# Attention feeding a gated feed-forward block: the order of the early loads, two sets of casts, and the first weights in two pieces

## The chip, the core and the metric

The kernel runs on one core of a Trainium2 chip. The metric is the device time of one execution in microseconds (us), as the median of several runs; lower is better. The engines named below are TensorE (PE, and PEld for its weight loads), VectorE (DVE), ScalarE (ACT), GpSimd (POOL) and SyncE (SP), which here does nothing but issue transfers. GpSimd issues transfers too, on a DMA queue of its own.

## What is computed

Causal attention with a forgetting bias, over 8 batches of 8 heads, 576 positions and head size 64, and a gated feed-forward block on its output:

```
scores = (q @ k^T) / 8
cum    = cumsum(max(s, 0))
scores = where(causal, scores + min(-(cum_i - cum_j), 0), -1e9)
attn   = softmax(scores);  o = attn @ v
x      = o, heads side by side                   # 4608 tokens x 512
g      = x @ w_gate                              # 512 x 1536
out    = (g * sigmoid(g) * (x @ w_val)) @ w_out  # 1536 x 512
```

Inputs and output are float32; the matmuls run in bfloat16.

## The kernel before

**Tiles.** The 64 heads are numbered 0 to 63 (`bh` or `kk`), eight to a batch, four to a head block (`hb` or `h`, 0 to 15). One load brings k or q of a head block into a float32 buffer (`rawk`, `rawq`, 576 KB each, three buffers in turn). One load of V is a batch (`rawv`, five chunks of up to 128 positions, one buffer only). `cast_one` makes bfloat16 copies `ck` and `cq` of a head block (L249); `cast_v` makes those of V into `vt` (L176). k and q must lie transposed in `kq`, of which there are two sets, taken in turn by head blocks. For head blocks 0 to 4 TensorE transposes (L291) and ScalarE (k, L318) and VectorE (q, L320) copy the result into `kq`; `prep_one(hb, i)` does one of the four pieces of that. From block 5 on the casts are written to memory and come back through transposing transfers.

Four more rows of `kq` come from the cumulative sums, by small transfers (`aug`, L190), so that the score matmul adds the bias by itself.

**A head.** `score_piece` does the score matmuls in four pieces (L367), the exponential on ScalarE (L380) and the causal masks on GpSimd (L383 on the 512 columns of the diagonal, L388 on the last 64). `av_piece` multiplies by V, with a column of ones for the softmax sum (L405); `av_out` divides (L421, L422). The result goes transposed into `XT`: for the first two batches by TensorE (L455), later through memory.

**The feed-forward block** takes 512 tokens at a time (`ffn_items`, nine such tiles, 36 items each): twelve times a gate group of four matmuls (L571), tanh on ScalarE (L576), a value group (L586) and two VectorE operations, then four output groups of twelve matmuls (L599). The weights lie in `wg`, `wv` (two halves of 768 columns each) and `wo` (two halves), loaded by GpSimd with a cast on the way (L336).

**What sets the order.** [...] the order is written out by hand. `first_batch` does batch 0 alone (heads 0 to 7), with the first loads placed after chosen heads. Then the main loop goes through the items of the feed-forward tiles and between them calls `pump`, which advances the generator `attn_items` (heads 8 and on) to a set position. While the first feed-forward tile runs, the position goes from 8 to 17.65, linearly from item 6 to item 36. `hook` places single actions after numbered items of the first tile.

Within `attn_items`, `PREP_AT[h]` says after which (head of the block, score piece) a piece of the next head block's preparation comes. `side(h, step)`, called after the second score piece of a head, places later loads and casts: the casts of V 1 at head 11, those of head block 5 at heads 13 and 14, loads of V 2 at heads 10 and 11, of head block 6 at head 12. `AV_AT` puts the output matmuls of heads 8 and 9 after the scores of head 12, those of 10 and 11 after 13, those of 12 and 13 after 14. Since there is one `rawv` buffer, the load of V 2 can't begin before all casts of V 1 are done.

On SyncE's queue the program's order before is: V 0; k, q 2; rows of block 2; k, q 3; rows of block 3; V 1; k, q 4; V 2; k, q 6; k, q 5.

Of the kernel before, what the change touches and what calls it, by code (L numbers as in the profile page):

```python
# [19 lines left out]
def kernel(  # L20
# [11 lines left out]
    nc = tc.nc  # L32
# [48 lines left out]
    NPE = 5  # L81
# [24 lines left out]
    with tc.manual_schedule():  # L106
# [41 lines left out]
        def load_one(hb, name, rs=(0, NR)):  # L148
            b, g = divmod(hb, 2)
            if rs[0] == 0:  # L150
                loaded[name, hb] = raw.tile([128, NR, J, D], FP32, tag="raw" + name, name="raw" + name)
            nc.sync.dma_start(  # L152
                loaded[name, hb][:, rs[0] : rs[1], :, :].rearrange("x r j d -> x r (j d)"),
                SRC[name][0][b, g * HB + 2 * rs[0] : g * HB + 2 * rs[1], :, :].rearrange(
                    "(r e) (p j) d -> (e p) r (j d)", e=2, j=J
                ),
            )

        def load_qk(hb):
            load_one(hb, "k")  # L160
            load_one(hb, "q")

        def load_v(b, cs):
            if 0 in cs:
                loaded["v", b] = raw.tile([128, NCH, H, D], FP32, tag="rawv", bufs=1, name="rawv")
            t = loaded["v", b]
            for c in cs:
                n = 128 if c < 4 else TAIL
                nc.sync.dma_start(  # L169
                    t[0:n, c, :, :],  # L170
                    v[b, :, c * 128 : c * 128 + n, :].rearrange("h p d -> p h d"),
                )
# [12 lines left out]
        def aug(hb, engs):  # L185
            for hh in range(HB):
                r, e = divmod(hh, 2)
                r0 = 64 * (1 - r)
                bh = hb * HB + hh
                engs[hh].dma_start(  # L190
                    KQ[hb % 2][r][r0 : r0 + 4, :, e * S : (e + 1) * S],
                    HL[bh : bh + 1, :, :, :],
                )
# [48 lines left out]
        def cast_one(hb, name, eng):  # L242
            cts[name, hb] = cp.tile([128, J, NR, D], BF16, tag="c" + name, bufs=2, name="c" + name)
            dst = cts[name, hb].rearrange("x j r d -> x r j d")
            src_t = loaded[name, hb]
            if eng is nc.scalar:
                nc.scalar.copy(dst, src_t)
            else:
                eng.tensor_copy(dst, src_t)  # L249
# [75 lines left out]
        def w_load(kind, j, h=None):  # L325
            dst = {"g": WG, "v": WV, "o": WO}[kind][j]
            if kind == "o":
                src_ap = moe_w_out[j * WKO * 128 : (j + 1) * WKO * 128, :].rearrange(
                    "(c p) n -> p c n", p=128
                )  # L330
            else:
                w = moe_w_gate if kind == "g" else moe_w_val
                lo, hi = (0, WCH) if h is None else (h * WCH // 2, (h + 1) * WCH // 2)
                src_ap = w[:, j * WCH + lo : j * WCH + hi].rearrange("(c p) n -> p c n", p=128)
                dst = dst[:, :, lo:hi]
            nc.gpsimd.dma_start(dst, src_ap)  # L336
# [101 lines left out]
        def x_out(pr):  # L438
            nc.gpsimd.dma_start(  # L439
                XS[pr].rearrange("(c p) d -> p c d", p=128), ots.pop(pr)  # L440
            )
# [6 lines left out]
        def x_pe(pr, eng=None):  # L448
            b, r = divmod(pr, H // 2)
            ot = ots.pop(pr)  # L450
            bs = take()
            ps = view16(bs, S)
            for c in range(NCH):
                n = 128 if c < 4 else TAIL
                nc.tensor.transpose(  # L455
                    ps[:, c * 128 : c * 128 + n], ot[0:n, c, :], ident[0:n, 0:n]
                )
            for lo, hi, at in x_parts(b):
                if eng is nc.scalar:
                    nc.scalar.copy(XT[:, r, at : at + hi - lo], ps[:, lo:hi])  # L460
                else:
                    nc.vector.tensor_copy(XT[:, r, at : at + hi - lo], ps[:, lo:hi])
            give(bs)
# [40 lines left out]
        def prep_one(hb, i):  # L504
            g, nm = divmod(i, 2)
            nm = ("k", "q")[nm]
            pe_transpose(hb, nm, g)
            for r in range(2):
                pe_out(hb, nm, g, r, nc.scalar if nm == "k" else nc.vector)

        PREP_AT = {
            2: {(1, 3): 0, (2, 1): 1, (2, 3): 2, (3, 1): 3},
            3: {(0, 3): 0, (1, 3): 1, (2, 1): 2, (2, 3): 3},
        }

        AV_AT = {
# [5 lines left out]
        def attn_items():  # L522
            for kk in range(H, BH + 2):
                h, step = divmod(kk, HB)
                if kk < BH:
                    if step == 3 and h + 2 < NPE:
                        cast_one(h + 2, "k", nc.gpsimd)
                        cast_one(h + 2, "q", nc.gpsimd)
                    if step == 0 and 3 < h + 1 < NPE:
                        aug(h + 1, GP4)  # L530
                    for ci in range(4):
                        score_piece(kk, ci)
                        if ci == 1:
                            side(h, step)
                        yield kk + 0.1 + ci / 8
                        if (step, ci) in PREP_AT.get(h, ()):
                            prep_one(h + 1, PREP_AT[h][step, ci])
                            yield kk + 0.1 + ci / 8
                for x in X_AT.get(kk, (kk - 2,)):
                    if x % 2 == 1 and H <= x < BH:  # L540
                        if x < XB * H:
                            x_pe(x // 2)
                            yield kk + 0.5
                        else:
                            x_in(x // 2)
                for p in AV_AT.get(kk, (kk - 1,)):
                    if H <= p < BH:
                        av_piece(p, (0, 1, 2))
                        yield kk + 0.6
                        av_piece(p, (3,))  # L550
                        yield kk + 0.7
                        av_piece(p, (4,))
                        av_out(p)
                        if p >= XB * H and p % 2 == 1:
                            x_out(p // 2)
                        yield kk + 0.8
# [101 lines left out]
            give(bs)  # L658

        def first_batch():  # L660
            wq = {1: (("g", 0), ("v", 0)), 4: (("g", 1),), 5: (("v", 1),)}
            tail = {
                6: ("a0", "a1"),
                7: ("a2", "a3", "a4", "x0", "a5", "x1", "a6", "a7", "x2", "w6", "x3", "w8"),
            }
            for h in range(H):
                for ci in range(4):
                    score_piece(h, ci)
                for w in wq.get(h, ()):
                    w_load(*w)  # L670
                if h == 1:
                    order = [(nm, g) for g in range(2) for nm in ("k", "q")]
                    for nm, g in order:
                        pe_transpose(1, nm, g)
                    for r in range(2):
                        for nm, g in order:
                            pe_out(1, nm, g, r, nc.vector)
                    for c in range(3, 5):
                        cast_v(0, c, nc.vector)
                if h == 2:  # L680
                    for c in range(3):
                        cast_v(0, c, nc.gpsimd)
                if h == 3:
                    aug(2, SP4)
                    load_qk(3)
                if h == 7:
                    aug(3, SP4)
                    load_v(1, range(5))
                    load_qk(4)
                    cast_one(2, "k", nc.gpsimd)  # L690
                    cast_one(2, "q", nc.gpsimd)
                    w_load("o", 0)
                    w_load("o", 1)
                for what in tail.get(h, ()):
                    i = int(what[1:])
                    if what[0] == "a":
                        av_piece(i, range(NCH))
                        av_out(i)
                    elif what[0] == "x":
                        x_pe(i, nc.scalar)  # L700
                    else:
                        keep_warm(i)
# [6 lines left out]
        def pump(upto):  # L709
# [9 lines left out]
            2: [lambda: prep_one(2, 1)],  # L719
            3: [lambda: prep_one(2, 2)],  # L720
            4: [lambda: prep_one(2, 3)],
            9: [lambda: cast_one(3, "k", nc.gpsimd), lambda: cast_one(3, "q", nc.gpsimd)],
            21: [lambda: load_qk(5)],
        }
        for tt in range(NTT):
            lo = H * (tt + 1) + LAGS[tt]
# [40 lines left out]
```

The softmax here doesn't subtract the row's maximum and nothing guards it: scores larger than these inputs give would overflow.

## Time and profile before

The time is 401.94 us, the median of three runs (400.12 to 403.02). The profiled execution has a span of 401.8 us at a mean granted TensorE clock of 0.987.

| engine | busy us | share of the span |
|---|---|---|
| PE | 373.3 | 93% |
| PEld | 207.3 | 52% |
| DVE | 241.5 | 60% |
| ACT | 214.3 | 53% |
| POOL | 192.4 | 48% |

Some single operations that the text below uses:

| operation | line | engine | mean ns |
|---|---|---|---|
| feed-forward matmul, 512 columns | L571, L586, L599 | PE | 381 to 383 |
| exponential of 128x512 | L380 | ACT | 504 |
| mask on 512 columns | L383 | POOL | 644 |
| cast of k of a head block | L249 | POOL | 1148 |
| issue of one weight load | L336 | POOL | 757 to 840 |

The page has a row per engine with its busy share in 40 equal slices of the span, one with the clock that TensorE was granted and one with the share of the 16 DMA engines. Beside it, the list of waits says for an engine how long it waited, in how many times, and for what; the timeline gives instructions in order of time, with the idle time ahead of each and what ended it in brackets; and the busy time can be had for any stretch. Times of matmuls overlap, since they are pipelined, and the record leaves out a few of them.

### The profile page before, as it was taken

The numbers are of one execution on the slowest core, as the hardware profiler recorded it, in microseconds if no ns is written. First come the engines' busy times: TensorE is split into PE (matmuls) and PEld (weight loads), VectorE is DVE, ScalarE is ACT, GpSimd is POOL, SyncE is SP. The second block draws the span as 40 slices with busy tenths as digits, with TensorE's granted clock in tenths as the row PEclk, the third lists the DMA queues.
The fourth block names the chain that finished last, engine by engine and source line by source line (L and its number), as shares of the span: only waits on it lengthen the run. The fifth ranks groups of instructions, "written<-read, shape, count | busy, mean of one in ns | idle before, by whom it ended". The sixth has DMA issues, their size and how long they took to land.

```text
span 401.8 us, 7873 instructions
## 1 busy us (share of the span) xinstructions
PE 373.3 (93%) x2943; PEld 207.3 (52%) x2994; DVE 241.5 (60%) x431; ACT 214.3 (53%) x411; POOL 192.4 (48%) x329
## 2 busy tenths in 40 slices
PE   4789979399999999999999999999999999999996
PEld 3575535255555555555555555555555554444442
DVE  7766756315885578627962795479627743842850
ACT  8576954245765665556555655565556522323321
POOL 7581436176578675667565756575542211001001
PEclk9999989979999999999999999999999999999999
DMA  7999975689685998899389939793531114002002
GB/s 248 223 268 207 197 185 125 234 213 244 153 185 148 278 288 176 204 286 232 106 197 277 232 112 190 217 208 104 97 127 27 23 25 135 2 22 82 2 0 105
DMA packets 100534, 64.18 MB, mean 160 GB/s; under 512 B 81888, under 2 KB 85824, under 8 KB 100496
## 3 DMA queue, kind: packets, MB, share of 16 engines
q1 hardware_dynamic: 90672, 45.23, 47.2%
q0 software_dynamic: 9680, 18.32, 17.1%
q8 instruction: 23, 0.38, 0.4%
q14 instruction: 15, 0.12, 0.1%
q10 hardware_dynamic: 144, 0.13, 0.1%
HBM read 37.90 MB, written 19.86 MB: 144 GB/s over the span
## 4 chain that ended last, share of the span: by engine, by line
PE 72%; DMA 9%; SPq 8%; issue 4%; DVE 2%; POOL 2%; ACT 2%; POOLq 0%; DVEq 0%; ACTq 0%
PE bank L599 20%; PE bank L571 18%; PE bank L586 18%; PE bank L367 8%; SPq L169 7%; PE bank L405 5%; DMA rawq<-in_q_dram 3%; DMA rawk<-in_k_dram 2%; DMA pk<-ks 2%; PE wide L367 2%; ACT pt L380 1%; SPq L152 1%; POOL vt L176 1%; DMA XT<-xs 1%; DMA kq<-HL 1%
## 5 line engine op out<-in xcount | busy, mean ns | idle before, releaser
L380 ACT ACTIVATE pt<-bank 128x512 bf16<-128x512 f32 x224 | 104.3, 504 | 52.4 <-PE bank L367 40.2
L578 DVE SCALAR_TENSOR_TENSOR pp<-th,bank 128x512 bf16<-128x512 bf16 x108 | 74.1, 686 | 74.5 <-ACT th L576 73.9
L571 PE MATMUL bank<-XT,wg 128*128 128x512 bf16 x409 | 110.5, 381 | 2.2 <-DMA XT<-xs 0.6
L586 PE MATMUL bank<-XT,wv 128*128 128x512 bf16 x421 | 110.0, 381 | 0.3
L576 ACT ACTIVATE th<-bank 128x512 bf16<-128x512 f32 x108 | 64.5, 597 | 79.3 <-PE bank L571 75.4
L599 PE MATMUL bank<-wo,ht 128*128 128x512 bf16 x415 | 103.5, 383 | 1.0 <-issue 0.2
L591 DVE TENSOR_TENSOR ht<-pp,bank 128x512 bf16<-128x512 bf16 x108 | 74.0, 685 | 9.8 <-PE bank L586 0.9
L367 PE MATMUL bank<-kq 128*128 128x128 bf16 (+4 forms) x504 | 66.7, 242 | 2.4 <-DVE kq L320 2.1
L367 PEld LDWEIGHTS <-kq 128*128 128x128 bf16 x576 | 47.3, 101 | 42.0 <-issue 6.5
L383 POOL TENSOR_SCALAR_AFFINE_SELECT pt<-pt 128x512 bf16<-128x512 bf16 x64 | 41.2, 644 | 43.4 <-ACT pt L380 42.8
L571 PEld LDWEIGHTS <-wg 128*128 128x128 bf16 x432 | 38.5, 98 | 36.9 <-issue 1.8
L599 PEld LDWEIGHTS <-ht 128*128 128x128 bf16 x432 | 38.7, 99 | 36.4 <-issue 1.1
L586 PEld LDWEIGHTS <-wv 128*128 128x128 bf16 x432 | 38.5, 98 | 35.5 <-issue 1.6
L405 PEld LDWEIGHTS <-pt 128*128 128x128 bf16 x960 | 41.8, 98 | 28.9 <-POOL pt L388 6.8
L405 PE MATMUL bank<-vt,pt 128*128 128x65 bf16 x840 | 43.3, 194 | 8.3 <-POOL pt L388 6.7
L439 POOL DMA_DIRECT2D xs<-ot x24 | 21.8, 910 | 58.9 <-DVE ot L422 58.9
L622 POOL DMA_DIRECT2D out_dram<-ysb x35 | 19.6, 562 | 60.9 <-ACT ysb L616 60.9
L616 ACT ACTIVATE ysb<-bank 128x512 f32<-128x512 f32 x35 | 20.9, 598 | 41.5 <-PE bank L599 38.5
L421 DVE RECIPROCAL rc<-bank 128x5 f32<-128x5 f32 x56 | 10.6, 190 | 40.0 <-PE bank L405 39.9
L190 POOL DMA_DIRECT2D kq<-HL x52 | 31.2, 602 | 2.3 <-PE bank L571 1.6
L422 DVE TENSOR_TENSOR ot<-bank,rc 128x320 bf16<-128x320 f32 x56 | 27.5, 492 | 1.9
L249 POOL CAST ck<-rawk 128x1152 bf16<-128x1152 f32 x14 | 16.1, 1148 | 19.3 <-DMA rawk<-in_k_dram 19.3
(66 smaller groups left out, 209.5 us busy)
## 6 DMA issues: line engine op xcount, KB each, us to landing
out_dram<-ysb POOLq DMA_DIRECT2D x35, 256.0 KB, 3.2
rawk<-in_k_dram SPq DMA_DIRECT2D x15, 576.0 KB, 4.8
rawq<-in_q_dram SPq DMA_DIRECT2D x15, 576.0 KB, 6.2
rawv<-in_v_dram SPq DMA_DIRECT2D x32, 256.0 KB, 4.6
xs<-ot POOLq DMA_DIRECT2D x24, 160.0 KB, 3.8
ks<-ck SPq DMA_DIRECT2D x11, 288.0 KB
qs<-cq SPq DMA_DIRECT2D x11, 288.0 KB, 3.9
wg<-in_moe_w_gate_dram POOLq DMA_DIRECT2D x2, 768.0 KB, 12.6
```

The lines of the kernel that those rows point to most:

```text
L169: nc.sync.dma_start(t[0:n, c, :, :], v[b, :, c * 128 : c * 128 + n, :].rearrange("h p d -> p h d"),)
L190: engs[hh].dma_start(KQ[hb % 2][r][r0 : r0 + 4, :, e * S : (e + 1) * S], HL[bh : bh + 1, :, :, :],)
L367: nc.tensor.matmul(sc[:, o : o + w], T[:, 1, e * S + 128 * tj : e * S + 128 * (tj + 1)], T[:, 0, e * S + lo : e * S + hi], start=True, sto ...
L380: nc.scalar.activation(pt[:, c0 : c0 + W], sc[:, 0:W], AF.Exp, scale=0.125)
L383: nc.gpsimd.affine_select(pt[:, 1088:1600], pt[:, 1088:1600], pattern=[[0, 4], [1, 128]], compare_op=ALU.is_ge, fill=zreg, base=0, channel ...
L405: nc.tensor.matmul(av[:, bi * (D + 1) : (bi + 1) * (D + 1)], pt[:, c0 : c0 + 128], VT[b % 2][:, tj, h, :], start=(tj == 0), stop=(tj == bi),)
L571: nc.tensor.matmul(pg, WG[j][:, c, f0 : f0 + 128], xt[:, c, :], start=(c == 0), stop=(c == 3),)
L576: nc.scalar.activation(th, pg, AF.Tanh, scale=0.5)
L578: nc.vector.scalar_tensor_tensor(pp, in0=th, scalar=1.0, in1=pg, op0=ALU.add, op1=ALU.mult)
L586: nc.tensor.matmul(pv, WV[j][:, c, f0 : f0 + 128], xt[:, c, :], start=(c == 0), stop=(c == 3),)
L591: nc.vector.tensor_mul(ht, pp, pv)
L599: nc.tensor.matmul(py, hts[ft][:, ts_ * 128 : (ts_ + 1) * 128], WO[ft // WKO][:, ft % WKO, :], start=(ft == 0), stop=(ft == NFT - 1),)
```

## The change

It has three parts, all in the first quarter of the run.

- **Loads and their order.** k, q of head block 3 are loaded after the rows of block 3 instead of before them, still ahead of V 1. k, q of head block 5 are loaded directly behind those of 4, instead of by a hook at item 21 of the first feed-forward tile. SyncE's order becomes: V 0; k, q 2; rows of block 2; rows of block 3; k, q 3; V 1; k, q 4; k, q 5; V 2; k, q 6.
- **Casts and preparation.** The casts of head block 3 come at item 6 instead of item 9, and block 3 is prepared at earlier places among heads 8 to 11. The casts of head block 4 move from the start of head 11, ahead of the casts of V 1, to the start of head 13, behind them; block 4 is prepared at later places among heads 12 to 15.
- **First weights in pieces.** The first half of the gate and of the value weights (768 columns each) is loaded as two pieces of 384 columns each; the first pieces are issued after head 1, as the whole was, the second after head 2.

It is for having each load land nearer to when it is used, so that a cast at the head of GpSimd's queue does not wait for data while others stand behind it.

```diff
         PREP_AT = {
-            2: {(1, 3): 0, (2, 1): 1, (2, 3): 2, (3, 1): 3},
-            3: {(0, 3): 0, (1, 3): 1, (2, 1): 2, (2, 3): 3},
+            2: {(0, 3): 0, (1, 3): 1, (2, 1): 2, (2, 3): 3},
+            3: {(1, 3): 0, (2, 1): 1, (2, 3): 2, (3, 1): 3},
         }
...
-                    if step == 3 and h + 2 < NPE:
-                        cast_one(h + 2, "k", nc.gpsimd)
-                        cast_one(h + 2, "q", nc.gpsimd)
+                    if step == 1 and 3 < h + 1 < NPE:
+                        cast_one(h + 1, "k", nc.gpsimd)
+                        cast_one(h + 1, "q", nc.gpsimd)
...
-            wq = {1: (("g", 0), ("v", 0)), 4: (("g", 1),), 5: (("v", 1),)}
+            wq = {1: (("g", 0, 0), ("v", 0, 0)), 2: (("g", 0, 1), ("v", 0, 1)), 4: (("g", 1),), 5: (("v", 1),)}
...
                 if h == 3:
                     aug(2, SP4)
-                    load_qk(3)
                 if h == 7:
                     aug(3, SP4)
+                    load_qk(3)
                     load_v(1, range(5))
                     load_qk(4)
                     cast_one(2, "k", nc.gpsimd)
                     cast_one(2, "q", nc.gpsimd)
+                    load_qk(5)
...
-            9: [lambda: cast_one(3, "k", nc.gpsimd), lambda: cast_one(3, "q", nc.gpsimd)],
-            21: [lambda: load_qk(5)],
+            6: [lambda: cast_one(3, "k", nc.gpsimd), lambda: cast_one(3, "q", nc.gpsimd)],
```

## The prediction

> **What bounds the kernel now.** I read the page's second part first, to see where TensorE is not full.
>
> ```profile
> PE   4789979399999999999999999999999999999996
> ...
> PEclk9999989979999999999999999999999999999999
> ```
>
> A digit covers 10.05 us. From 90 us to the end PE stands at 9 in every slice but the last; the holes are all in the first nine slices, and the two dips of the granted clock lie in or just behind two of them. The edit touches nothing but those slices, so its worth is read there. The list of waits, PE alone, says what ended each hole after the start-up:
>
> ```profile
> PE bank L405 <- POOL pt L388: 6.7, 1, 6.7
> ...
> PE bank L367 <- DVE kq L320: 2.1, 1, 2.1
> PE bank L405 <- POOL vt L176: 1.6, 3, 0.9
> ```
>
> Three waits, not many: one of 6.7 us, one of 2.1 us, and a broken one of 1.6 us. The timeline puts them at 74.2, 51.9 and 59.4 us. I asked for the engines' busy time in the stretches that these cut out:
>
> ```profile
> 32.00:51.90 19.90, 19.53 (x136) 10.96 (x140) 14.53 (x21) 16.10 (x32) 4.79 (x8) 1.00 1.19 202
> 51.90:54.20 2.30, 0.20 (x3) 0.04 (x2) 2.16 (x5) 1.03 (x3) 0.00 (x0) 1.00 1.05 214
> 54.20:59.40 5.20, 5.14 (x25) 2.43 (x27) 2.27 (x4) 1.74 (x4) 2.36 (x3) 0.67 0.52 188
> 59.40:61.70 2.30, 0.74 (x11) 0.43 (x9) 0.41 (x1) 2.04 (x4) 2.30 (x5) 1.00 0.00 0
> 61.70:74.20 12.50, 12.39 (x153) 8.07 (x154) 9.05 (x19) 6.72 (x13) 4.92 (x10) 1.00 0.76 204
> 74.20:80.90 6.70, 0.03 (x2) 0.01 (x1) 0.49 (x1) 0.00 (x0) 2.50 (x5) 0.85 0.49 185
> 80.90:86.20 5.30, 5.08 (x24) 2.65 (x25) 0.69 (x2) 2.01 (x5) 4.90 (x9) 0.54 0.57 178
> 86.20:100.00 13.80, 13.70 (x135) 8.14 (x137) 5.97 (x13) 7.97 (x17) 8.66 (x15) 1.00 0.99 245
> ```
>
> The columns after the stretch and its length are PE, PEld, DVE, ACT and POOL busy, then granted clock, DMA share and GB/s. PE is 98 to 99% busy at full clock outside the holes. So the removable loss is: 2.1 idle (2.30 - 0.20); then 5.20 x (1 - 0.67) = 1.7 on a slow clock; 1.6 idle (2.30 - 0.74); 6.7 idle; then 5.30 x (1 - 0.54) = 2.4 on a slow clock. **Sum 14.5 us.** From 86 us on PE is the bound, so what is won before stays won.
>
> Why the holes exist is in GpSimd's timeline:
>
> ```profile
> 56.78 1.15 POOL L249 CAST ck<-rawk 128x1152 bf16<-128x1152 f32 x1 [7.56 <-DMA rawk<-in_k_dram]
> 58.18 1.15 POOL L249 CAST cq<-rawq 128x1152 bf16<-128x1152 f32 x1 [0.26 <-DMA rawq<-in_q_dram]
> 59.28 0.64 POOL L383 TENSOR_SCALAR_AFFINE_SELECT pt<-pt 128x512 bf16<-128x512 bf16 x1
> 59.86 2.83 POOL L176 CAST vt<-rawv 128x512 bf16<-128x512 f32 x5
> ...
> 78.40 1.14 POOL L249 CAST ck<-rawk 128x1152 bf16<-128x1152 f32 x1 [11.76 <-DMA rawk<-in_k_dram]
> 79.48 1.17 POOL L176 CAST vt<-rawv 128x512 bf16<-128x512 f32 x2
> 80.61 0.24 POOL L388 TENSOR_SCALAR_AFFINE_SELECT pt<-pt 128x64 bf16<-128x64 bf16 x1
> ```
>
> First block: the cast of k 4 stands ahead of the casts of V 1 and waits for its own load. Second block: the cast of k 5 stands ahead of the mask of a head that PE needs, and k 5 was issued only at 69.52 us, as SyncE's timeline shows, behind V 2 and k, q 6. V 2 in turn waited for the casts of V 1. The 2.1 us hole is the last of the four transposed copies of block 3 (VectorE, L320, 53.36 us), placed directly ahead of the scores that read it.
>
> [...] The trace's packet records agree: from 33 to 41 us the packets of V 1 (256 bytes) and of the weights (1536 bytes) start at 112 per us each, from 42 to 51 us at 150 each, though one packet is several times the other; V alone runs at about 950 per us. So V 1 crawls until the weights are through (51.7 us). [...] Here a hole of 2.1 us was enough; the slow stretches after it and after the 6.7 us one are those of 0.67 and 0.54 above. [...]
>
> **The change, part by part.**
>
> *Preparation of block 3 half a head to a head earlier* (L512). Its four pieces move to (0,3), (1,3), (2,1), (2,3). The last copy then lies before head 11's scores, 3 to 4 us ahead of head 12's. The 2.1 us hole and its 1.7 us of slow clock go. It needs k 3 cast by about 41 us (head 8 starts at 39.25). Cost of the moved transposes: none, the same instructions beside the same work.
>
> *k, q 3 behind the augmented rows of block 3* (L685 to L687). Issued at 26.9 us instead of 20.1. In between, SyncE waits for scores to free a buffer and its queue runs dry; the weights then have the DMA engines alone (130 packets per us in 22 to 24 us), so bytes are conserved. Against weights, k and q got 73 packets per us each side (28 to 31 us); 512 packets take 7.0 us. First packet about 2.5 us after issue: landed by 37 to 38 us. The casts, moved to item 6, find GpSimd idle (9.03 us idle ahead of 40.60): k by 36, q by 39. In time.
>
> *V 1 behind them.* It starts near 37 instead of 31 us. Weights left then: about 384 packets of 1536 bytes and 1536 of 1024 bytes, that is 384/112 + 1536/150 = 13.7 us, to 50.6. V 1 has 1920 of its 4608 packets by then; the rest takes 2688/950 = 2.8 us: through at 53.5 us, the same as before (53.5). The total of DMA work decides, not its order.
>
> *Halved first weights* (L661). Twice the packets of half the size. By the packets' median durations (134 ns for 1536 bytes, 96 ns for 1024) a 768-byte one is estimated at 77 ns, so two cost 154 against 134: 15% of the 1024 packets' 7.9 us, +1.2 us of DMA time as one end, 0 as the other, if the engines overlap it. I take 0.6, so V 1 is through at 54 us, landed at 55. On GpSimd two more issues of 0.78 us; behind them wait the casts of V 0 (ended 20.9, needed at 24.3), later masks and the cast of block 2 (ended 29.96, needed at 32.7). Covered.
>
> *Casts of 4 behind V 1* (L525). V 1's casts no longer wait for k 4 (56.78). They end about 0.6 us after the last chunk lands: 55.7. PE reaches head 8's output matmuls at 59.4 - 2.1 - 1.7 - 0.2 (a transpose group that moves away) = 55.4, and needs the last chunk half a microsecond later. The 1.6 us shrinks to 0 to 1, or 3 if V 1 is late; I take 0.7. k, q 4 then land near 57.5 and 58.5, cast by about 60; block 4's first transposes, moved to (1,3), are reached at about 60.3. I allow 0.3 there.
>
> *k, q 5 directly behind 4.* From 57.5, 3.1 us alone at 165 packets per us (as in 72 to 77 us): landed by 61.5, 17 us sooner than 78.4. V 2 follows, freed by the casts of V 1 at 56 instead of 62.7: its first two chunks land near 64. The DMA lull from 58 to 64 us is filled. GpSimd then does cast 4 (2.3), a mask (0.6), cast of k 5 (1.14), two V casts (1.17), the mask L388 of head 13: done near 65.3. PE wants it at 74.2 - 2.1 - 1.7 - 1.6 = 68.8. Slack 3.5 us: the 6.7 and the 2.4 go. Allowance 0.4 for a late chunk.
>
> **Sum:** 401.9 - 14.5 + 0.7 + 0.3 + 0.4 = **388.8 us**.
>
> **The rivals.** *V 1 still late:* the halves cost their full 1.2 us and the dry queue loses some bandwidth, V 1 lands at 58, PE waits 3 us and pays 1.7 of slow clock: 401.9 - 14.5 + 4.7 + 0.4 = 392.5. For it: V 1 starts 6 us later and depends wholly on the weights' end. Against: DMA share above 1.05 all the way from 12 to 54 us. *The wait moves to head 13:* V 2 behind k, q 5 keeps its first chunks until 68, casts block the mask as before, PE waits 3 and loses 2.4: 401.9 - 14.5 + 0.7 + 5.4 = 393.5. [...] against: 3.5 us of slack. *Slower:* k, q 3 are starved as V 1 was (23 us for one load), land near 50; block 3's preparation, now earlier, stops PE for 9 us and 2.4 of clock, and V 1 behind it lands at 60 for another 6: 401.9 - 14.5 + 17.4 = 404.8. Against it: packets of 2304 bytes against 1536 in equal turns have never starved in the trace.
>
> **How the numbers follow.** Forecast 0.55, V 1 late 0.22, head 13 0.12, slower 0.08, other 0.03. The forecast's own width is 386.5 to 391; adding both middle rivals, each give or take 2, the range is 386.3 to 396.0. Faster by over 1% (below 397.9): 0.55 + 0.22 + 0.12 less a little for a rival that goes deeper = 0.88; slower 0.08; same 0.04.
>
> **What would show it.** Right: no PE wait above 1.5 us after 32 us; no slow clock after the start; the casts of V 1 ahead of those of 4 and ending by 56 us; the cast of k 5 with no long wait; DMA busy from 58 to 64 us. Wrong: a PE wait on kq L320 or on transposes at 41 us (k 3 late), on vt L176 above 2 us (V 1 late), or on pt L388 near 68 us (V 2 late).

## The result

The changed kernel takes 389.65 us (median of four runs, 389.12 to 390.27), the kernel before 402.15 us in the same comparison (400.12 to 403.02). The ratio is 0.9697, 95% interval 0.9657 to 0.9736: faster by 3%, or 12.5 us. The forecast was 388.8.

The page of the changed kernel, the rows of TensorE and of its granted clock by fortieths of the span (9.7 us each now):

```profile
PE   3789999999999999999999999999999999999995
...
PEclk9999999999999999999999999999999999999999
```

The holes after the start are gone, and with them the dips of the clock. TensorE's list of waits, in us in total, times, and the longest:

```profile
PE bank L405 <- POOL vt L176: 0.7, 1, 0.7
...
PE bank L571 <- DMA XT<-xs: 0.6, 1, 0.6
PE bank L291 <- POOL ck L249: 0.5, 1, 0.5
```

The waits of 6.7 us (pt L388) and 2.1 us (kq L320) are not in it at all; of the broken 1.6 us for V 1, 0.7 is left; 0.5 us is new, for k 4 at its later place. Busy time by stretches, with the same columns as before the change:

```profile
32.00:51.90 19.90, 19.15 (x135) 10.63 (x136) 16.82 (x25) 16.38 (x32) 6.08 (x10) 1.00 1.18 219
51.90:60.00 8.10, 7.33 (x68) 4.22 (x68) 5.13 (x10) 5.02 (x12) 5.98 (x12) 1.00 1.01 316
60.00:75.00 15.00, 14.32 (x169) 9.25 (x170) 9.26 (x19) 9.30 (x19) 10.89 (x18) 1.00 1.05 290
75.00:86.00 11.00, 10.89 (x107) 6.46 (x107) 5.28 (x11) 6.75 (x16) 7.92 (x14) 1.00 1.14 255
```

TensorE is idle for 0.75 + 0.77 + 0.68 + 0.11 = 2.3 us of these 54, at full clock throughout. The DMA share (above 1 when on average more than 16 packets are under way at a time), which was 0.00 in one stretch around 60 us and 0.49 to 0.57 around 80, stays at 1.0 and above: the lull is filled. GpSimd's timeline shows why:

```profile
54.79 0.62 POOL L176 CAST vt<-rawv 128x512 bf16<-128x512 f32 x1 [1.04 <-DMA rawv<-in_v_dram]
55.86 0.61 POOL L176 CAST vt<-rawv 64x512 bf16<-64x512 f32 x1 [0.45 <-DMA rawv<-in_v_dram]
...
56.61 2.38 POOL L190 DMA_DIRECT2D kq<-HL  x4
...
59.78 1.14 POOL L249 CAST ck<-rawk 128x1152 bf16<-128x1152 f32 x1
60.87 1.14 POOL L249 CAST cq<-rawq 128x1152 bf16<-128x1152 f32 x1
61.97 0.63 POOL L383 TENSOR_SCALAR_AFFINE_SELECT pt<-pt 128x512 bf16<-128x512 bf16 x1
62.55 1.13 POOL L249 CAST ck<-rawk 128x1152 bf16<-128x1152 f32 x1
63.83 0.62 POOL L176 CAST vt<-rawv 128x512 bf16<-128x512 f32 x1
64.84 0.62 POOL L176 CAST vt<-rawv 128x512 bf16<-128x512 f32 x1 [0.39 <-DMA rawv<-in_v_dram]
65.40 0.24 POOL L388 TENSOR_SCALAR_AFFINE_SELECT pt<-pt 128x64 bf16<-128x64 bf16 x1
```

The last two chunks of V 1 are cast as they land and end at 56.5 us (62.7 before). The casts of k, q 4 and of k 5, which waited 7.56 and 11.76 us for their loads, no longer wait for them, and the mask of head 13 is done at 65.6 instead of 80.9 us.

One part of the gap between the two profiles lies ahead of the holes. The spans differ by 14.0 us (401.8 and 387.8), of which 1.7 us lie ahead of the first gate matmul:

```profile
32.07 1.02 PE L571 MATMUL bank<-XT,wg 128*128 128x512 bf16 x3 [0.17 <-ACT XT L460]
```

is the kernel before, and the changed kernel has

```profile
30.34 1.02 PE L571 MATMUL bank<-XT,wg 128*128 128x512 bf16 x3 [0.17 <-ACT XT L460]
```

The order of TensorE's instructions up to there is the same in both. What differs is when its clock came up: in the profile before, the nine score matmuls at 13.00 us and again those at 16.21 us took 1.49 us, in the other those at 13.14 us took 0.95. The trace's clock records agree. They begin with full clock at 17.5 us in the one and at 12.5 us in the other; ahead of its first record a view prints full clock, so the row of the page does not show this. From the first gate matmul on, the difference is 12.3 us.

### The profile page after: what moved, and what is told of

Its sections match the earlier page's. It is cut to its first block, busy times and chain, and to the rows that moved or that the text cites. A ratio compares the mean times of both kernels' runs of the same rounds, so it can differ in the third digit from the quotient of the medians.

```text
span 387.8 us, 7880 instructions
## 1 busy us (share of the span) xinstructions
PE 367.4 (95%) x2944; PEld 204.2 (53%) x2994; DVE 242.7 (63%) x431; ACT 214.4 (55%) x411; POOL 195.2 (50%) x331
## 4 chain that ended last, share of the span: by engine, by line
PE 78%; SPq 7%; DMA 4%; DVE 4%; issue 3%; ACT 1%; POOL 1%; POOLq 0%; DVEq 0%; ACTq 0%
PE bank L599 21%; PE bank L571 20%; PE bank L586 20%; PE bank L367 9%; SPq L169 7%; PE bank L405 6%; DMA rawq<-in_q_dram 3%; DVE kq L320 1%; PE wide L367 1%; DMA XT<-xs 1%; DMA xs<-ot 1%; PE one L405 1%; PE one L305 1%; DVE pp L578 1%; DVE ht L591 1%
## 5 line engine op out<-in xcount | busy, mean ns | idle before, releaser
L578 DVE SCALAR_TENSOR_TENSOR pp<-th,bank 128x512 bf16<-128x512 bf16 x108 | 74.1, 687 | 71.1 <-ACT th L576 70.4
L586 PE MATMUL bank<-XT,wv 128*128 128x512 bf16 x407 | 109.1, 379 | 1.3
L367 PEld LDWEIGHTS <-kq 128*128 128x128 bf16 x576 | 46.2, 98 | 38.5 <-issue 5.3
L367 PE MATMUL bank<-kq 128*128 128x128 bf16 (+4 forms) x504 | 65.9, 240 | 0.4 <-DVE ht L591 0.2
L586 PEld LDWEIGHTS <-wv 128*128 128x128 bf16 x432 | 38.4, 98 | 34.9 <-issue 0.8
L388 POOL TENSOR_SCALAR_AFFINE_SELECT pt<-pt 128x64 bf16<-128x64 bf16 x64 | 17.0, 265 | 20.3 <-ACT pt L380 20.2
```

The source lines that it names most:

```text
L367: nc.tensor.matmul(sc[:, o : o + w], T[:, 1, e * S + 128 * tj : e * S + 128 * (tj + 1)], T[:, 0, e * S + lo : e * S + hi], start=True, sto ...
L578: nc.vector.scalar_tensor_tensor(pp, in0=th, scalar=1.0, in1=pg, op0=ALU.add, op1=ALU.mult)
L586: nc.tensor.matmul(pv, WV[j][:, c, f0 : f0 + 128], xt[:, c, :], start=(c == 0), stop=(c == 3),)
```

## The experiments

Two theories were set against each other. **A, one chain:** the three holes hang on one chain of transfers and casts (weights, V 1, k 4, casts of V 1, V 2, k 5), so each part's worth depends on the others. **B, separate holes:** each part takes away its own hole and the gains add. Ratios are to the kernel before in the same comparison.

### One part alone

```diff
                     cast_one(2, "q", nc.gpsimd)
+                    load_qk(5)
...
-            21: [lambda: load_qk(5)],
```

> The kernel before, with the load of k, q 5 alone moved behind that of 4. Theory A (one chain of transfers and casts feeds all three holes, so the parts don't add): the hole at head 13 and its slow clock go (9.1 us), the waits of 2.1 and 1.6 us stay: 393 us. Theory B (three holes with a cause each, the gains add): the same, 402.1 - 9.1 = 393. Rival C (V 2 is what the mask of head 13 waits for, not k 5): a wait of PE for pt L388 of 3 us or more stays near 74 us and the time is above 396.

Measured: 396.77 us, ratio 0.9852 (0.9810 to 0.9894), a gain of 5.5 and not 9.1. The wait for pt L388 is gone, so rival C falls: it was k 5, not V 2. TensorE's waits in this kernel:

```profile
PE bank L405 <- POOL vt L176: 2.9, 3, 2.2
PE bank L367 <- DVE kq L320: 2.1, 1, 2.1
...
PE bank L571 <- DMA XT<-xs: 1.7, 2, 1.1
```

No slow clock followed the 2.1 us hole in this profile (1.00 from 54 to 61 us), but the time that this saved was spent waiting for V 1 (2.9 instead of 1.6). A wait of 1.1 us for a transposed transfer at 130.7 us is new: a stage that had slack while TensorE was late has a little less now. Part of the miss lies in how it was worked out: the 9.1 us were read from the profile of a run of 403.55 us, 1.3 above the median that the kernel before has here (402.24), and the first gate matmul came 0.6 us later in this profile (32.63 against 32.07). From that matmul on, the profiles differ by 7.4 us. Of the 1.7 us missing there, the two waits (1.3 and 1.1 us more) less the slow clock that stayed away (1.7) give 0.7; the other 1.0 stays open.

```diff
-                    if step == 3 and h + 2 < NPE:
-                        cast_one(h + 2, "k", nc.gpsimd)
-                        cast_one(h + 2, "q", nc.gpsimd)
+                    if step == 1 and 3 < h + 1 < NPE:
+                        cast_one(h + 1, "k", nc.gpsimd)
+                        cast_one(h + 1, "q", nc.gpsimd)
...
-            3: {(0, 3): 0, (1, 3): 1, (2, 1): 2, (2, 3): 3},
+            3: {(1, 3): 0, (2, 1): 1, (2, 3): 2, (3, 1): 3},
```

> The kernel before, with the casts of 4 alone behind those of V 1 (and the preparation of 4 moved with them); the load of k, q 5 stays at its late place. Theory A: the casts of V 1 end near 56 us instead of 62.7, so V 2, k, q 6 and k, q 5 all come some 6 to 7 us sooner and the hole at head 13 shrinks from 6.7 to about 1 us without its load being touched: about 393 us. Theory B: only the broken wait of 1.6 us goes: 400.5 us, the wait for pt L388 stays at 6 us or more.

Measured: 394.73 us, ratio 0.9797 (0.9746 to 0.9848), 1.7 us above A's 393. B said 400.5. GpSimd's timeline of this kernel:

```profile
54.94 1.29 POOL L176 CAST vt<-rawv 128x512 bf16<-128x512 f32 x2 [0.61 <-DMA rawv<-in_v_dram]
...
70.23 1.14 POOL L249 CAST ck<-rawk 128x1152 bf16<-128x1152 f32 x1 [7.86 <-DMA rawk<-in_k_dram]
```

V 1 is done at 56.2 us and k 5, whose load was not touched, is issued at 62.95 us instead of 69.52 and cast at 70.23 instead of 78.40: two casts put behind five others moved another load 6.6 us and its cast 8.2 us forward through the single buffer of V. The wait for pt L388 is 2.4 us, more than the 1 expected, and VectorE's product at L578 holds TensorE 1.0 us at 146.35.

```diff
-            2: {(1, 3): 0, (2, 1): 1, (2, 3): 2, (3, 1): 3},
+            2: {(0, 3): 0, (1, 3): 1, (2, 1): 2, (2, 3): 3},
...
-            9: [lambda: cast_one(3, "k", nc.gpsimd), lambda: cast_one(3, "q", nc.gpsimd)],
+            6: [lambda: cast_one(3, "k", nc.gpsimd), lambda: cast_one(3, "q", nc.gpsimd)],
```

> The kernel before, with the earlier preparation and casts of block 3 alone. Theory A: the 2.1 us hole and its slow clock go, but PE only reaches the output matmuls of head 8 some 4 us sooner and waits there for the casts of V 1, which hang on k 4's landing at 56.8; the wait for vt L176 grows from 1.6 to 4 to 5 us and k 5 lands when it did: 401 to 402 us, within 0.5% of before. Theory B: 402.1 - 3.8 = 398.3 us.

Measured: 401.73 us, ratio 0.9993 (0.9971 to 1.0015): no change, where B said 398.3. The wait for kq L320 is gone from TensorE's list, and this stands in its place:

```profile
PE bank L405 <- POOL pt L388: 3.9, 1, 3.9
...
PE bank L291 <- POOL ck L249: 2.9, 1, 2.9
PE bank L405 <- POOL vt L176: 2.6, 3, 2.1
PE bank L586 <- DMA wv<-in_moe_w_val_dram: 2.3, 1, 2.3
```

TensorE came sooner and waited longer: 2.9 us for k 4's cast and 2.6 for V 1, while k 5's cast began at 78.39 us as before (78.40). The last line stood in neither theory: the first value weights landed only at 33.4 us. This profile is of a run of 404.13 us, one of the slowest of its twenty, with two stretches of 6.8 us at half clock; it shows where the time goes better than how much.

### One part undone in the changed kernel

```diff
-            2: {(0, 3): 0, (1, 3): 1, (2, 1): 2, (2, 3): 3},
+            2: {(1, 3): 0, (2, 1): 1, (2, 3): 2, (3, 1): 3},
```

> The changed kernel, with the preparation of block 3 put back to its later places (its cast stays at item 6). Theory A: the hole of 2.1 us and a slow clock of 1.7 us come back ahead of head 12's scores, but PE then no longer waits for V 1 (0.7) and k 4 (0.5): 389.65 + 3.8 - 1.2 = 392.2 us. Theory B: 393.5 us. If the preparation's place was worth nothing once the casts are in order: 389.7 us.

Measured: 392.99 us, ratio 0.9735 (0.9673 to 0.9797). The 2.1 us wait is back, with a slow stretch behind it (clock 0.83 from 50 to 60 us), and no wait for V 1 or k 4:

```profile
PE bank L367 <- DVE kq L320: 2.1, 1, 2.1
```

By the medians the edit that brought 0.3 us alone (0.07%) is worth 3.3 here, between what A and B said. But the intervals of this ratio and of the changed kernel's (0.9657 to 0.9736) overlap, the ratios differ by 1.5 us only, and one of the four runs took 389.02. So the wait is shown, and what it costs in this kernel is not.

```diff
-                    load_qk(5)
...
+            21: [lambda: load_qk(5)],
```

> The changed kernel, with the load of k, q 5 put back to item 21. Theory A: V 2 (freed near 56.5), k, q 6 and then k, q 5 pass in about 5 + 3 + 2 us, so k 5 lands near 67 to 68, its cast and two V casts end near 70, and PE, which wants the mask of head 13 at 68.2, waits 1.5 to 3 us, with or without a slow clock: 391.5 to 394 us. Theory B (this load's place was worth the whole 6.7 + 2.4): 398.7 us.

Measured: 394.40 us (392.41 to 396.55), ratio 0.9846 (0.9802 to 0.9890): 0.4 us above the upper end of A by the median. Against the changed kernel's ratio it is 389.65 x 0.9846 / 0.9697 = 395.6, give or take 2.5: beyond A, but still short of B's 398.7. In the profile, of the slowest of the four runs, 3.4 us of half clock (worth 1.7) stand behind the wait (clock 0.83 from 70 to 80 us):

```profile
PE bank L405 <- POOL pt L388: 3.2, 1, 3.2
```

```diff
-                    if step == 1 and 3 < h + 1 < NPE:
-                        cast_one(h + 1, "k", nc.gpsimd)
-                        cast_one(h + 1, "q", nc.gpsimd)
+                    if step == 3 and h + 2 < NPE:
+                        cast_one(h + 2, "k", nc.gpsimd)
+                        cast_one(h + 2, "q", nc.gpsimd)
...
-            3: {(1, 3): 0, (2, 1): 1, (2, 3): 2, (3, 1): 3},
+            3: {(0, 3): 0, (1, 3): 1, (2, 1): 2, (2, 3): 3},
```

> The changed kernel, with the casts of 4 ahead of those of V 1 again (and the preparation of 4 moved with them). Theory A: k 4 is landed near 56, so the casts of V 1 start near 58 to 59 instead of 50 and end near 62; PE waits for vt L176 some 3.5 to 4.5 us and pays up to 1.7 us of slow clock, k 5 is there already and head 13 costs nothing more: 394 to 396 us. Theory B: only the 1.6 us comes back: 391.3 us. A rival (V 2 now comes too late for head 13 as well): 398 us or more.

Measured: 397.57 us, ratio 0.9913 (0.9882 to 0.9943), 1.6 us beyond the upper end of A. TensorE's timeline shows what I had left out:

```profile
58.99 0.45 PE L291 MATMUL bank<-ident,ck 128*128 128x128 bf16 x5 [3.32 <-POOL ck L249]
61.63 0.27 PE L405 MATMUL bank<-vt,pt 128*128 128x65 bf16 x2 [2.18 <-POOL vt L176]
```

With the casts, block 4's preparation moves forward too, and now TensorE itself stands at its transposes until k 4 is cast. That wait of 3.3, 2.7 for V 1, and half clock behind them (0.66 from 60 to 70 us, worth 3.4 us) less the 1.2 of waits that it replaces make 8.2; measured 7.9 by the medians. The rival named 398 us or more, not far from this, but its wait, for pt L388 at head 13, is not in the list.

Together, gains over the kernel before in per cent, each from its own ratio. The last four rows also contain the two other edits, the weights in pieces and the later k, q 3:

| parts | gain |
|---|---|
| preparation of 3 | 0.1 |
| load of 5 | 1.5 |
| casts of 4 | 2.0 |
| preparation of 3, load of 5 | 0.9 |
| preparation of 3, casts of 4 | 1.5 |
| load of 5, casts of 4 | 2.7 |
| all | 3.0 |

Intervals are 0.3 to 0.6 to either side (0.2 for the first). The parts don't simply add: the preparation of 3 and the load of 5 make 1.6 apart and 0.9 together. For the load of 5 and the casts of 4 (3.5 apart, 2.7 together) the gap lies inside the intervals. With only one of these two the preparation brings nothing that these runs can tell. B falls by the casts of 4 alone (394.73 where it said 400.5) and by the preparation alone (401.73 where it said 398.3).

### Weights in pieces and k, q 3

```diff
-            wq = {1: (("g", 0, 0), ("v", 0, 0)), 2: (("g", 0, 1), ("v", 0, 1)), 4: (("g", 1),), 5: (("v", 1),)}
+            wq = {1: (("g", 0), ("v", 0)), 4: (("g", 1),), 5: (("v", 1),)}
```

> The changed kernel, with the first gate and value weights loaded whole again. Prediction's step: the halves cost 0 to 1.2 us of DMA time, 0.6 taken, and bring nothing: V 1's last chunk lands 0.6 us sooner, the PE wait for vt L176 falls from 0.7 to near 0: 389.0 to 389.7 us. Rival (the smaller first pieces let the first feed-forward groups start): 390.5 us or more, with a PE wait on L571 or L586 near 30 to 33 us.

Measured: 389.59 us, ratio 0.9727 (0.9700 to 0.9755): the same time as with the pieces.

```diff
                     aug(2, SP4)
+                    load_qk(3)
...
                     aug(3, SP4)
-                    load_qk(3)
```

> The changed kernel, with the load of k, q 3 put back ahead of the rows of block 3. Theory of conserved DMA work: the same total of packets has to pass before V 1 is through, so V 1's casts end within 1 us of 56.5 and the time is within 0.3% of 389.65. Rival (k, q 3 in front holds the first weights up, or the later load was what brought V 1 in time): V 1's casts end more than 2 us later and the time is above 391.5 us.

Measured: 390.65 us, ratio 0.9754 (0.9722 to 0.9787). The casts of V 1 end at 56.8 us, against 56.5, as the total of transfers says. The time is 1.0 us above that of the kernel with whole weights in the same comparison (389.25 to 390.10 there, 389.69 to 391.61 here); in this profile TensorE's waits for V 1 come to 1.4 us instead of 0.7. Both edits undone at once:

> The changed kernel, with both parts undone that each alone were worth 0 to 1 us: whole first weights and k, q 3 ahead of the rows of block 3. Theory D (each of the two alone brings the first value weights in time): now they land near 33.3 us as before, and PE waits for wv at its first L586 up to 2.3 us, the more the sooner TensorE's clock got going: 390.5 to 392.5 us. Theory E (neither part is worth anything): 389.7 to 390.7, no wait for wv.

Measured: 390.85 us (389.83 to 394.02), ratio 0.9748 (0.9703 to 0.9793). The wait for the value weights is there, in a profile whose first gate matmul came at 31.94 us:

```profile
PE bank L586 <- DMA wv<-in_moe_w_val_dram: 0.5, 1, 0.5
```

In the kernels where either edit stands, it is in no list of waits, even where the first gate matmul came at 29.74 us (with the pieces; with the later load alone it came at 32.66). The packet records settle it for both: the last packet of the value weights that TensorE needs first ended at 32.3 us here, at 28.8 with the later k, q 3 alone and at 27.2 with the pieces alone. So D holds as a mechanism; its time lies inside the intervals and is not shown.

### Two attempts at a better version

```diff
-                    w_load("o", 0)
-                    w_load("o", 1)
...
+            10: [lambda: w_load("o", 0)],
+            14: [lambda: w_load("o", 1)],
```

> The changed kernel, with the loads of the output weights put off from before the main loop to items 10 and 14 of the first feed-forward tile. Theory of equal turns (V 1 crawls beside whatever weights are under way): without 1536 packets in its way V 1 is through by about 45 us instead of 54, its casts start at head 11 without waiting and PE's waits for V 1 (0.7) and k 4 (0.5) go; the output weights land by about 57 us, wanted at 62: 388.4 us. Rival (the total of DMA work decides, whatever the order): V 1's casts still end near 56 us and the time stays at 389.6; or the output weights come late and PE waits for wo near 62 us: above 390.

Measured: 389.92 us (388.42 to 390.69), ratio 0.9709 (0.9672 to 0.9745). The mechanism holds: the last packet of V 1 came at 46.2 us, where it was 54.4 in the changed kernel, the five casts run in one piece, and both waits are gone.

```profile
51.86 2.83 POOL L176 CAST vt<-rawv 128x512 bf16<-128x512 f32 x5
```

The time is the same, though. In this profile the first gate matmul came at 32.25 us, 1.9 later than in the changed kernel's, and then those waits need no cure: with whole weights it came at 32.66 us and neither wait was there either.

```diff
+        warm_up(34)
         cast_half(0, "k", 0, nc.scalar)
...
                 pe_transpose_half(0, nm, g, 0)
+        warm_up(4)
...
                 pe_out(0, nm, g, 1, eng)
+        warm_up(4)
```

`warm_up(n)` takes a score bank and does n matmuls of the identity with itself.

> The changed kernel, with 34 dummy matmuls on TensorE while it waits for the first casts and 4 more in each of two short gaps, nothing left out. Theory F (in the first 20 us the time varies with when TensorE's clock is granted in full, which was 9 to 18 us in the profiles so far): the clock is full before the first scores, the first gate matmul comes at 29.5 to 30 us in every run, and the median falls by 0.3 to 1.5 us to 388.2 to 389.4. Rival (the start hangs on ScalarE's exponentials and the loads): 389.6 +- 0.4, the first gate matmul where it was.

Measured: 392.07 us, ratio 0.9762 (0.9723 to 0.9800), 2.4 us slower than the changed kernel. Theory F's first claim holds, since the clock was full ahead of the first scores at 11.62 us; the other two fail, and the rival's 389.6 is not met either. Stretches of this kernel:

```profile
6.00:9.00 3.00, 1.99 (x28) 1.43 (x26) 2.93 (x5) 2.44 (x5) 1.68 (x5) 1.00 0.96 351
9.00:13.00 4.00, 1.83 (x22) 1.34 (x23) 3.04 (x5) 1.59 (x3) 2.79 (x4) 0.95 0.52 153
13.00:17.00 4.00, 3.65 (x36) 3.16 (x36) 1.66 (x4) 2.47 (x5) 2.33 (x5) 0.63 1.04 232
```

The clock records give full clock from 5.8 to 12.6 us and half clock from there to 16.0. TensorE was busy for only 1.8 of the 4 us from 9 to 13 us. That this brought the fall is not shown: in the kernel before it was busy for 2.1 of the 4 us from 18 to 22 us and kept full clock. The first gate matmul came at 31.70 us. Much of the loss lies far behind the start: from 100 to 200 us TensorE is busy for 97.3 us, in the changed kernel for 99.0. At 142.80 us it waits 0.95 us for VectorE's L578, which it doesn't there. Why an edit of the first 20 us does this stays open.

> Both of the last two additions on the changed kernel: output weights put off, and the dummy matmuls at the start. If both theories hold the gains add, since one is ahead of 32 us and the other behind it: 387.0 to 388.2 us.

Measured: 391.21 us, ratio 0.9751 (0.9712 to 0.9791): there are no gains to add. None of these versions is shown to beat the changed kernel.

## Why the prediction was right

**The holes and their sum.** Right as to what is lost: all three waits went or shrank as said, and TensorE stays the bound from there to the end. From the first gate matmul on, the trace gives 12.3 us, where 14.5 less 1.4 of allowances was forecast. The idle time above what the old kernel had outside its holes (0.4 + 0.1 + 0.1 + 0.2) is 2.3 - 0.8 = 1.5 us. That this is close to the 1.4 is luck. The waits for V 1 and k 4 are there in the two profiles of an early start, with the first gate matmul at 30.34 us and at 29.74 (k, q 3 put back in front). In two kernels that keep all of the chain and started like the kernel before, at 32.66 (whole weights) and 31.94 us (both undone), neither wait is there, and the gain from the first gate matmul on is 14.0 and 13.6 us. Nor was the early start worth its 1.7 us: those two spans are 388.4 and 388.1 us against 387.8. What TensorE won ahead of the loads, it mostly waited off again. Two terms of the sum were sized from a single profile, the slow stretches of 1.7 and 2.4 us. They vary: the same 2.1 us hole had none behind it in the kernels with the load of 5 or the casts of 4 alone (clock 1.00 from 54 to 61 and from 52 to 60 us). That profile's run took 403.55 us, 1.4 above the median, and the sum of 14.5 was read from it.

**k, q 3.** Forecast cast by 36 and 39 us; the casts end at 35.4 and 38.9. Equal numbers of packets from the two queues, from which this was worked out, were found: from 29.4 to 34 us, 74 packets per us of k and q and 75 of weights. That the times agree so well is luck in part: the load was issued at 25.2 us, 1.7 sooner than forecast, but its first packet came 3.8 us after that and not 2.5, and its packets took 8.1 us and not 7.0.

**V 1 and its casts.** Forecast through at 54 us, cast at 55.7, with 0.7 us of TensorE's time; the last packet came at 54.4 (54.2 in the kernel before, where the forecast read 53.5), the casts ended at 56.5, half a microsecond past the sign set for them, and the wait was 0.7. In these two kernels the total of transfers did decide.

**Casts of 4 and k 5.** Forecast cast by 60 us with a wait of 0.3; the casts end at 62.0, the wait is 0.5. The step left out what GpSimd does between: it issues the rows of block 4 from 56.61 to 58.99 us, shown above, ahead of the cast of k 4. The mask of head 13 was forecast at 65.3, found at 65.6, and nobody waits: the 0.4 allowed was not needed.

**The weights in pieces.** The size of a packet's time was right (77 ns estimated, 79 found in the packet records), but the step saw only a cost. In the kernel before, the first value weights landed almost exactly when TensorE reached them (its first L586 was at 33.33 us); with an earlier start it waits for them (2.3 us in the kernel with the preparation of 3 alone). The pieces, or the later k, q 3, take that limit away. My steps had nothing about the start of the run.

**The rivals.** V 1 late, and the wait moved to head 13, both would have shown as waits of 3 us; there are 0.7 and 0. k, q 3 were not starved. A wait at head 13 was not far off: with the load of 5 put back in the changed kernel there is one of 3.2 us, though for k 5 and not for V 2. What the prediction did not say is that its sum stood only because all the parts were changed together: had I been asked for one of them, the same sum of holes would have misled me, as theory B was.

## What to carry to other kernels

Waits that follow each other on the critical engine may be one chain seen three times: before adding up what it costs to remove them, ask for each what its releaser waited for, and whether an earlier arrival would only wait longer. The worst hole here came of a mask of 0.24 us behind a cast that waited 11.76: ScalarE's last exponential ahead of it ended at 72.97 us, and GpSimd took the mask only at 80.61, after the casts written ahead of it. So put a cast of data still under way behind everything that is ready and wanted. A single buffer carries such a delay on: the next load started when the last cast ended (V 2 was issued at 62.72 us before and at 56.50 after, each time within 0.05 us of the last cast of V 1).

## What the runs showed of the hardware

- While V 1 and the weights were both under way, their packets started in nearly equal numbers, though those of the weights were four to six times the size. In the kernel before, 113.0 per us of V 1 (256 bytes) and 112.3 of the weights (1536 bytes) from 33 to 40 us, 149.6 and 150.2 (1024 bytes) from 42 to 50; in the changed kernel, 111.5 and 112.5 from 37 to 39 us, 150.3 and 150.5 from 43 to 49.
- The clock of TensorE in the first 20 us varied from profile to profile in kernels with the same TensorE instructions there: the records of full clock begin at 17.5 us in the kernel before and at 12.5 in the changed one, and the first gate matmul came at 32.07 and 30.34 us. Over these profiles it came at 29.74 to 32.66. With dummy work ahead of the first stage the clock was full from 5.8 to 12.6 us and half from there to 16.0.
- The same hole of 2.1 us was followed by 3.4 us at half clock in two profiles (the kernel before, from 55.06 to 58.47 us; the changed one with the old preparation, clock 0.83 from 50 to 60 us) and by none in two others (the load of 5 alone, 1.00 from 54 to 61 us; the casts of 4 alone, 1.00 from 52 to 60). That such a hole was enough, as the forecast has it, held in two of four. Other stretches of half clock were of 6.83 us in the kernel before (from 78.95 us) and, worked out from the granted clock, of 3.4 us in the changed kernel with the late load of 5 and 6.8 us in the one with the casts of 4 first.
